# Decode attention with a gated feed-forward on one core: key transposes moved to VectorE in 32x32 blocks, and wider products at the end

## The chip, the cores and the metric

One NeuronCore of a Trainium2 chip runs the whole kernel; the other cores are idle. The metric is device time in microseconds: the median of the runs, lower is better. A profile of one execution comes with it. In what follows PE is TensorE, PEld its weight loads, DVE is VectorE, ACT is ScalarE, POOL is GpSimd and SP is SyncE, which here only issues loads.

## The reference

Two tokens (B = 2) go through one layer: attention over the last 4096 cached positions, 32 query heads on 8 key/value heads of 128, and beside it a gated feed-forward of width 1792. All data is float32.

```python
W = min(4096, max(256, Sk // 4))              # 4096 of 32768 cached positions
xn = _layernorm(x)
q = (xn @ wq).reshape(B, Sq, 32, 128)
scores = einsum("bhqd,bhkd->bhqk", q, k[last W]) * 128 ** -0.5
o = einsum("bhqk,bhkd->bhqd", softmax(scores), v[last W])
attn = o.reshape(B, Sq, 4096) @ wo
gate, up = xn @ W_gate, xn @ W_up
h = (gate * (gate > 0)) * up
return x + attn + h @ W_down
```

Nearly all bytes are read once: wq 8 MB, W_gate, W_up and W_down 3.5 MB each, keys and values 32 MB each, wo 8 MB, 95 MB in all.

## The kernel before, in words

**Loads.** Every large load is issued by SP's queue into a ring of four slots of 32 KB per partition (`RING`, line 17). A slot takes one load of about 4 MB; SP waits at a load until the last reader of its slot is done. In order of the program: x (three small loads, issued by ACT), `wq` in two halves (line 136), `w_gate`, `w_up` (226), and then keys and values. `load_kv` (114) fetches 4096 positions of two heads, 64 partitions for each, one 32 KB row per partition. There are four groups g (two batch rows times two halves of the heads), each with two key and two value loads (a = 0, 1). `load_down` (95) comes as 13 rows per partition and a rest of 128 rows in two small loads into a tile `wx`; `wo` comes in one load of 4 MB and four of 2, 1.25, 0.5 and 0.25 MB (498).

**Start.** Layernorm statistics of x run on DVE and POOL, the normalised row is spread to columns by 16 products (212), and 32 products of 512 columns form q (222). q is transposed and laid out in `qz` (228 to 241). Then the gate and up products run (243 to 257), and h is transposed into `hT` (283 to 293).

**A group.** `transposes` (308) turns the keys on PE, 128x128 at a time, into PSUM; `evacuate` (304) copies four of these at once to the tile `kt`, by turns on ACT and DVE. `scores` (322) multiplies `qz` by `kt`, 512 columns at a time, into four 32-row strips of one PSUM bank. `softmax` (335) takes the maxima, spreads them, runs Exp on ACT over a doubled view, turns the probabilities on PE (373) and masks them on DVE (374). `values` (386) multiplies them by the value tile; `gather` (404) and `finish` (414) sum the parts. `kwork` (432) writes out by hand how PE interleaves a key tile's transposes with the softmax of the group before. The keys of group g are worked ahead of the values of group g - 1, and loads are issued in that order.

**End.** After the last group, `project` (478) multiplies h by `w_down` and the heads by `wo`, each as four products of 128 columns into four strips of `y_ps`; the four late pieces of `wo` let the last products start as each piece lands. `y_ps` is copied to `yo` and stored (501 to 503).

Each engine works in the order of the program; a wait at its head holds all that is behind it.

Of the kernel before, what the change touches and what calls it, by code (L numbers as in the profile page):

```python
# [9 lines left out]
F32 = mybir.dt.float32  # L10
# [10 lines left out]
def kernel(  # L21
# [28 lines left out]
    S1 = W // (Q * 512)  # L50

# [7 lines left out]
    ring = ctx.enter_context(tc.tile_pool(name="ring", bufs=RING))  # L59
    ktp = ctx.enter_context(tc.tile_pool(name="ktp", bufs=2))  # L60
    work = ctx.enter_context(tc.tile_pool(name="work", bufs=2))
    ps_kt = ctx.enter_context(tc.tile_pool(name="ps_kt", bufs=3, space=PSUM))
# [5 lines left out]
    def load(name, src, shape):  # L68
        t = ring.tile(shape, F32, name=name, tag="ring")
        nc.sync.dma_start(t, src)  # L70
        return t


    def load_wq(m):
        src = wq[m * 2 * P:(m + 1) * 2 * P, :].rearrange("(p k) f -> p k f", p=P)
        return load(f"wq{m}", src, [P, 2, HQ * DH])

    def load_ff(w, name):
        return load(name, w.rearrange("(p k) f -> p k f", p=P), [P, KC, F])
# [6 lines left out]
    FM = 13  # L86
    KX = 4
    LEFT = 0
    FX = F - P * FM
    RX = (FX - 8 * LEFT) // (8 * KX)  # L90
    SX = RX + (LEFT > 0)
    MQ = P * FM // Q
    assert 8 * KX * RX + 8 * LEFT == FX

    def load_down():
        t = ring.tile([P, FM, D], F32, name="wd", tag="ring")
        wx = ktp.tile([P, SX, D], F32, name="wx", tag="kT")
        nc.gpsimd.memset(wx[0:64], 0.0)  # L98
        nc.sync.dma_start(
            t.rearrange("p k e -> p (k e)"), w_down[0:P * FM, :].rearrange("(p k) e -> p (k e)", p=P)  # L100
        )
        row = P * FM
        for b in range(2):
            src = bass.AP(
                tensor=w_down.tensor, offset=w_down.offset + row * D,
                ap=[[RX * D, KX], [KX * RX * D, 4], [1, RX * D]],
            )
            nc.sync.dma_start(wx[32 * b:32 * b + 4 * KX, 0:RX].rearrange("p k e -> p (k e)"), src)
            row += 4 * KX * RX
        for i in range(LEFT):  # L110
            nc.sync.dma_start(wx[i:32:4, RX], w_down[row + 8 * i:row + 8 * i + 8, :])
        return t, wx

    def load_kv(cache, name, g, a):
        r, b = divmod(g, B)
        base = cache[b, r * C + 2 * a, SK - W:SK, :]
        run = J * DH
        src = bass.AP(
            tensor=cache.tensor, offset=base.offset, ap=[[run, PK], [SK * DH, 2], [1, run]]
        )  # L120
        return load(f"{name}{g}_{a}", src, [P, run])
# [14 lines left out]
    wqt = [load_wq(m) for m in range(2)]  # L136
# [4 lines left out]
    NSLOT = C * S1  # L141
    qz = const.tile([P, NG, NSLOT * 36], F32, name="qz")
    nc.gpsimd.memset(qz, 0.0)
    ones = const.tile([1, 1], F32, name="ones")
# [4 lines left out]
    hT = const.tile([P, FM + SX, B, 16], F32, name="hT")  # L149
    nc.gpsimd.memset(hT, 0.0)  # L150
    hx = const.tile([32, SX, 64], F32, name="hx")
    nc.gpsimd.memset(hx, 0.0)
# [8 lines left out]
    spread = const.tile([HR, NE, HR, NE], F32, name="spread")  # L161
    nc.gpsimd.memset(spread, 0.0)
    for e in range(NE):
        nc.gpsimd.tensor_copy(spread[:, e, :, e], ident[0:HR, 0:HR])


    pick = const.tile([P, 4, 24], F32, name="pick")
    nc.gpsimd.memset(pick, 0.0)
    nc.vector.tensor_reduce(
        out=pick[:, :, 8:16], in_=ident.rearrange("p (q u k) -> p u k q", q=Q, u=4), op=ALU.add, axis=AX.X  # L170
    )


    HK = 2 * REP
    by_h = const.tile([P, NP, HK], F32, name="by_h")
    nc.vector.tensor_reduce(
        out=by_h, in_=ident.rearrange("p (q a s k) -> p a k q s", q=Q, a=NP, s=S1), op=ALU.add, axis=AX.XY
    )

    half_of = const.tile([P, 2], F32, name="half_of")  # L180
    nc.vector.tensor_reduce(
        out=half_of, in_=ident.rearrange("p (y h) -> p h y", h=2), op=ALU.add, axis=AX.X
    )
    own = const.tile([P, 2, REP], F32, name="own")
    nc.vector.tensor_copy(own, half_of[:, :, None].to_broadcast([P, 2, REP]))
# [22 lines left out]
    xt_ps = ps_1.tile([P, 2, KC, 32], F32, name="xt_ps", tag="misc")  # L208
    for kc in range(KC):
        m, k = divmod(kc, 2)  # L210
        for o, cols in ((0, xn.rearrange("r (m p k) -> r m k p", m=2, k=2)[:, m, k]), (1, xn.rearrange("r (p k) -> r k p", k=KC)[:, kc])):
            nc.tensor.matmul(xt_ps[:, o, kc, :], cols, rep.rearrange("r s b -> r (s b)"), start=True, stop=True)  # L212
    xnT = const.tile([P, 2, KC, 32], F32, name="xnT")
# [4 lines left out]
    for kc in range(KC):  # L218
        for r in range(R):
            for c in range(C):  # L220
                n = r * C + c
                nc.tensor.matmul(  # L222
                    q_ps[r][32 * c:32 * c + 32, :], xnT[:, 0, kc, :], wqt[kc // 2][:, kc % 2, n * 512:(n + 1) * 512],
                    start=(kc == 0), stop=(kc == KC - 1),
                )
    gw = load_ff(w_gate, "wg")
    uw = load_ff(w_up, "wu")
    for r in range(R):
# [3 lines left out]
        for i in range(REP):  # L232
            nc.tensor.transpose(
                qt[:, i].rearrange("p c s b -> p (c s b)"), qs[:, i * P:(i + 1) * P], ident
            )
        for b in range(B):
            dst = qz[:, r * B + b].rearrange("p (a s h k) -> p a s h k", a=NP, s=S1, h=2)
            for h in range(2):
                nc.vector.tensor_copy(
                    dst[:, :, :, h, 0:REP], qt[:, :, h::2, 0:S1, b].rearrange("p i a s -> p a s i")  # L240
                )
# [4 lines left out]
    x_ps = ps_1.tile([32, 2, FX], F32, name="x_ps", tag="o0")  # L246
    for h, dst, wt in ((0, g_ps, gw), (1, u_ps, uw)):
        for kc in range(KC):
            for c in range(Q):
                nc.tensor.matmul(  # L250
                    dst[32 * c:32 * c + 32, :], xnT[:, 1, kc, :], wt[:, kc, c * MQ:(c + 1) * MQ],
                    start=(kc == 0), stop=(kc == KC - 1),
                )
        for kc in range(KC):
            nc.tensor.matmul(
                x_ps[:, h], xnT[:, 1, kc, :], wt[:, kc, Q * MQ:], start=(kc == 0), stop=(kc == KC - 1)
            )
# [9 lines left out]
    gx = work.tile([32, 2, FX], F32, name="gx", tag="qs")  # L267
    nc.scalar.copy(gx[:, 0], x_ps[:, 0])
    nc.vector.scalar_tensor_tensor(gx[:, 1], gx[:, 0], 0.0, gx[:, 0], op0=ALU.is_gt, op1=ALU.mult)
    part = 4 * KX * RX  # L270
    for b in range(2):
        g_in, u_in = (
            a[:, b * part:(b + 1) * part].rearrange("p (j e s) -> p e j s", j=4, e=KX) for a in (gx[:, 1], x_ps[:, 1])
        )
        nc.vector.tensor_tensor(
            hx[:, 0:RX, 32 * b:32 * b + 4 * KX].rearrange("p s (e j) -> p e j s", j=4), g_in, u_in, op=ALU.mult
        )
    for i in range(LEFT):
        lo = 2 * part + 8 * i
        nc.vector.tensor_tensor(  # L280
            hx[:, RX, i:32:4], gx[:, 1, lo:lo + 8], x_ps[:, 1, lo:lo + 8], op=ALU.mult
        )
    ht_ps = ps_1.tile([P, FM + SX, B], F32, name="ht_ps", tag="misc")
    for k in range(FM):
        for c in range(Q):
            nc.tensor.matmul(
                ht_ps[32 * c:32 * c + 32, k], hh[:, k], ident[:, 32 * c:32 * c + B], start=True, stop=True
            )
    for k in range(SX):
        m = 64 if k < RX else 32  # L290
        nc.tensor.matmul(ht_ps[0:m, FM + k], hx[:, k, 0:m], ident[0:32, 0:B], start=True, stop=True)
    nc.vector.tensor_copy(hT[:, 0:FM, :, 0], ht_ps[:, 0:FM])
    nc.vector.tensor_copy(hT[0:64, FM:FM + RX, :, 0], ht_ps[0:64, FM:FM + RX])
    if LEFT:
        nc.vector.tensor_copy(hT[0:32, FM + RX, :, 0], ht_ps[0:32, FM + RX])
# [3 lines left out]
    HW = W // S1  # L299
    ss, pts, rls = {}, {}, {}  # L300
    kts, osb = {}, {}
    turn = [0]

    def evacuate(dst, src):
        (nc.vector.tensor_copy if turn[0] % 2 else nc.scalar.copy)(dst, src)  # L305
        turn[0] += 1

    def transposes(g, a, s1, kt_in):

        kt = ktp.tile([P, 2, HW], F32, name=f"kT{g}_{a}_{s1}", tag="kT")  # L310
        kts[g, a, s1] = kt
        for n in range(2 * Q):
            pk = ps_kt.tile([P, 512], F32, name=f"pk{g}_{a}_{s1}_{n}", tag="kt")
            for u in range(4):
                j = 8 * Q * s1 + 4 * n + u
                nc.tensor.transpose(pk[:, u * P:(u + 1) * P], kt_in[:, j * P:(j + 1) * P], ident)  # L316
            evacuate(
# [214 lines left out]
```

## Time and profile before

| | |
|---|---|
| median of 3 runs | 231.29 us (231.12 to 231.61) |
| the profiled execution | 231.43 us, its span 229.6 us |
| PE, PEld, DVE, ACT busy | 185.4, 114.7, 67.2, 46.9 us |
| bytes read | 94.90 MB, 413 GB/s over the span |
| instructions | 4149, of them 1876 matmuls and 1876 weight loads |

The span runs from the first to the last instruction; 1.8 us of the execution lie outside it. A busy PE is not a PE at its peak, since matmuls overlap one another. "DMA share" is the mean busy share of the 16 DMA engines. A float32 product is two matmul instructions in the rows (a transpose is one).

### The profile page before, as it was taken

What the parts mean: (1) busy time and instruction counts of PE and PEld (TensorE: products, weight loads), DVE (VectorE), ACT (ScalarE), POOL (GpSimd) and SP (SyncE); (2) the same over time, 40 slices, a digit from 0 to 9 for tenths busy, and PEclk for the clock granted to TensorE, in tenths of its full rate; (3) what the DMA queues carried; (4) which work ended last, traced back from release to release, by engine and by line L of the source; (5) the groups of instructions that cost most, each with busy time, mean ns of one, the idle gap of its engine ahead of it and who ended that gap; (6) DMA issues with size and microseconds to landing.
All of it is one profiled execution on the core that took longest, in us unless ns stands there. A gap on an engine that the chain in (4) does not pass through costs nothing.

```text
span 229.6 us, 4149 instructions
## 1 busy us (share of the span) xinstructions
PE 185.4 (81%) x1876; PEld 114.7 (50%) x1876; DVE 67.2 (29%) x135; ACT 46.9 (20%) x80; POOL 8.2 (4%) x25
## 2 busy tenths in 40 slices
PE   0059961779999899997799699889979973988794
PEld 0052231259666583663484566458446532247682
DVE  0320021034444570441472143157124224001000
ACT  0020100004344451440351233045023202010000
POOL 8100000000000000000000000000000300000000
PEclk9999999577999999999999799999999999599678
DMA  7999999999999999999999999999999999999981
GB/s 274 451 428 408 454 410 437 422 451 442 405 425 451 415 417 445 442 411 420 457 417 432 428 440 414 434 445 414 422 440 437 417 428 440 423 442 414 410 364 49
DMA packets 3824, 95.15 MB, mean 414 GB/s; under 512 B 434, under 2 KB 448, under 8 KB 704
## 3 DMA queue, kind: packets, MB, share of 16 engines
q1 hardware_dynamic: 3796, 94.90, 96.7%
q8 instruction: 14, 0.23, 0.4%
q14 instruction: 2, 0.02, 0.0%
q10 hardware_dynamic: 12, 0.00, 0.0%
HBM read 94.90 MB, written 0.00 MB: 413 GB/s over the span
## 4 chain that ended last, share of the span: by engine, by line
DMA 54%; PE 41%; DVE 2%; issue 1%; ACT 1%; ACTq 0%; POOL 0%; DVEq 0%
DMA k<-in_A_k_cache_dram 37%; PE pk L316 21%; DMA wo<-in_A_wo_dram 13%; PE s L329 7%; PE y_ps L480 5%; DMA x<-in_A_x_dram 4%; PE o L393 3%; PE q_ps L222 3%; PE xt_ps L212 2%; ACT p L362 1%; PE pp L373 0%; ACTq L135 0%; PE oa L409 0%; DVE stats L189 0%; DVE kT L305 0%
## 5 line engine op out<-in xcount | busy, mean ns | idle before, releaser
L316 PE MATMUL pk<-ident,k 128*128 128x128 f32 x512 | 67.9, 286 | 6.0 <-DMA k<-in_A_k_cache_dram 5.9
L316 PEld LDWEIGHTS pk<-ident,k 128*128 128x128 f32 x512 | 57.9, 146 | 20.9 <-issue 16.7
L305 DVE COPY kT<-pk 128x512 f32<-128x512 f32 x64 | 44.2, 691 | 52.1 <-PE pk L316 46.2
L305 ACT COPY kT<-pk 128x512 f32<-128x512 f32 x64 | 37.5, 585 | 69.5 <-PE pk L316 69.5
L393 PE MATMUL o<-v,pt 128*32 128x512 f32 x256 | 32.5, 641 | 0.0
L329 PE MATMUL s<-kT,qz 128*32 128x512 f32 x256 | 30.9, 598 | 0.0
L393 PEld LDWEIGHTS o<-v,pt 128*32 128x32 f32 x256 | 11.3, 117 | 15.7 <-issue 10.9
L212 PE MATMUL xt_ps<-rep,xn 2*128 2x32 f32 x16 | 3.7, 400 | 13.9 <-DVE xn L206 13.9
L329 PEld LDWEIGHTS s<-kT,qz 128*32 128x32 f32 x256 | 7.1, 109 | 11.9 <-issue 11.5
L305 DVE COPY on<-o 128x512 f32<-128x512 f32 x4 | 2.8, 692 | 30.5 <-PE o L393 30.5
L409 PE MATMUL oa<-on,pick 128*16 128x128 f32 x64 | 8.3, 273 | 4.1 <-DVE on L305 3.3
L480 PE MATMUL y_ps<-wo,oT 128*17 128x128 f32 x256 | 10.3, 329 | 1.6 <-DMA wo<-in_A_wo_dram 1.6
L409 PEld LDWEIGHTS oa<-on,pick 128*16 128x16 f32 x64 | 5.8, 97 | 11.3 <-DVE on L305 7.0
L250 PE MATMUL u_ps<-wu,xnT 128*32 128x416 f32 x32 | 5.8, 901 | 6.1 <-DMA wu<-in_B_W_up_dram 6.1
L212 PEld LDWEIGHTS xt_ps<-rep,xn 2*128 2x128 f32 x16 | 3.6, 320 | 13.9 <-issue 13.9
L222 PE MATMUL q_ps<-wq,xnT 128*32 128x512 f32 x64 | 9.7, 777 | 0.5 <-DVE xnT L214 0.5
L480 PEld LDWEIGHTS y_ps<-wo,oT 128*17 128x17 f32 x256 | 8.1, 119 | 3.6 <-DMA wo<-in_A_wo_dram 2.6
L305 ACT COPY on<-o 128x512 f32<-128x512 f32 x4 | 2.3, 586 | 27.0 <-PE o L393 27.0
L98 POOL MEMSET wx<- 64x2048 f32 x1 | 1.8, 1804 | 169.1 <-PE s L329 169.1
L362 ACT ACTIVATE p<-s,nm 128x1024 f32<-128x1024 f32 x4 | 4.5, 1114 | 13.1 <-DVE nm L357 13.1
L374 DVE TENSOR_TENSOR pt<-pp,own 128x512 f32<-128x512 f32 x8 | 5.4, 689 | 2.6 <-PE pp L373 2.6
L373 PE MATMUL pp<-ident,p 128*128 128x128 f32 x32 | 4.9, 280 | 1.7 <-ACT p L362 1.5
(83 smaller groups left out, 68.2 us busy)
## 6 DMA issues: line engine op xcount, KB each, us to landing
k<-in_A_k_cache_dram SPq DMA_DIRECT2D x8, 4096.0 KB, 23.9
v<-in_A_v_cache_dram SPq DMA_DIRECT2D x8, 4096.0 KB, 28.3
wq<-in_A_wq_dram SPq DMA_DIRECT2D x2, 4096.0 KB, 21.7
wo<-in_A_wo_dram SPq DMA_DIRECT2D x1, 4096.0 KB
wg<-in_B_W_gate_dram SPq DMA_DIRECT2D x1, 3584.0 KB, 29.8
wu<-in_B_W_up_dram SPq DMA_DIRECT2D x1, 3584.0 KB, 39.3
wd<-in_B_W_down_dram SPq DMA_DIRECT2D x1, 3328.0 KB
wo<-in_A_wo_dram SPq DMA_DIRECT2D x1, 2048.0 KB
```

Source lines behind the costliest of these rows:

```text
L212: nc.tensor.matmul(xt_ps[:, o, kc, :], cols, rep.rearrange("r s b -> r (s b)"), start=True, stop=True)
L222: nc.tensor.matmul(q_ps[r][32 * c:32 * c + 32, :], xnT[:, 0, kc, :], wqt[kc // 2][:, kc % 2, n * 512:(n + 1) * 512], start=(kc == 0), stop ...
L250: nc.tensor.matmul(dst[32 * c:32 * c + 32, :], xnT[:, 1, kc, :], wt[:, kc, c * MQ:(c + 1) * MQ], start=(kc == 0), stop=(kc == KC - 1),)
L305: (nc.vector.tensor_copy if turn[0] % 2 else nc.scalar.copy)(dst, src)
L316: nc.tensor.transpose(pk[:, u * P:(u + 1) * P], kt_in[:, j * P:(j + 1) * P], ident)
L329: nc.tensor.matmul(ss[g][32 * q:32 * q + 32, :], qz[:, g, 32 * n:32 * n + 32], kt[:, h, q * 512:(q + 1) * 512], start=(a == 0 and s1 == 0 ...
L362: nc.scalar.activation(p, both, AF.Exp, bias=nm, scale=SCALE, accum_out=l)
L373: nc.tensor.transpose(pp[:, u], pv[:, lo:lo + P], ident)
L374: nc.vector.tensor_tensor(pts[g][:, jh].rearrange("p n u k -> p u n k"), pp.rearrange("p u (n k) -> p u n k", k=HK), own.rearrange("p h i ...
L393: nc.tensor.matmul(o[32 * q:32 * q + 32, :], pts[g][:, jh, n].rearrange("p u k -> p (u k)"), v[:, lo:lo + 512], start=(s1 == 0 and jh == 0 ...
L409: nc.tensor.matmul(oa[g], pick[:, u, 8 - 8 * a:24 - 8 * a], ons[a][:, u], start=(a == 0 and u == 0), stop=(a == NP - 1 and u == 3),)
L480: nc.tensor.matmul(y_ps[32 * e:32 * e + 17, :], lhsT.rearrange("p b s -> p (b s)")[:, 0:17], w[:, e * P:(e + 1) * P], start=False, stop=stop,)
```

## The change: what it does

- **Keys.** PE no longer turns keys. DVE transposes each key tile in 32x32 blocks, four instructions of 128x2048 elements for each load, from the ring straight into `kt`. `qz` is laid out to fit (new `spot`, `qT`, `rq` and 16 small copies for each half of the heads); `scores` runs in four 32-row strips, two at a time.
- **Probabilities.** Exp runs over 512 columns, not 1024. Two products with a permutation (`perm`) put the rows in order, and one DVE transpose of 128x1024 writes `pts`. A mask now follows the value products (`gather`, on DVE), and one product, not four, gathers them; `finish` adds a reduction.
- **Order.** Within one loop step a group's keys and values are loaded k, k, v, v and worked in that order. `keep_busy` adds two PE products without a use at each group's start. `kwork` and the interleaving are gone.
- **Ring.** One tile of the same size, cut by `place`. `wq` is one load of 64 KB per partition over two slots; `w_down` is one load of 14 rows per partition, so that `wx`, `hx` and `x_ps` go. The first half of `wo` comes in two loads.
- **End.** Products with `w_down` and most of `wo` have 512 columns, each into the next of four 32-row strips of `y4` (`slot`). `y4` is copied by DVE and folded into `y_ps` by four products; the last eight products of `wo` keep four times 128 columns (`quarters`). x is loaded again (`xr`).

```diff
-    def load_wq(m):
-        src = wq[m * 2 * P:(m + 1) * 2 * P, :].rearrange("(p k) f -> p k f", p=P)
+    ring = const.tile([P, RING * RW], F32, name="ring")
+    def place(cols):
+        lo = taken[0] % RING * RW
+        taken[0] += -(-cols // RW)
+        return ring[:, lo:lo + cols]
+    def load_rows(w):
+        t = place(KC * w.shape[1])
+        nc.sync.dma_start(t, w.rearrange("(p k) f -> p (k f)", p=P))
...
+    def scores(g, a, kt_in):
+        for s1 in range(S1):
+            kt = ktp.tile([P, JH, CB, KL, 2], F32, name=f"kT{g}_{a}_{s1}", tag="kT")
+            for n in range(2):
+                lo = JH // 2 * n
+                j = JH * s1 + lo
+                nc.vector.transpose(
+                    kt[:, lo:lo + JH // 2].rearrange("p j c k h -> p (j c k h)"),
+                    kt_in[:, j * DH:(j + JH // 2) * DH],
+                )
+            for cb in range(CB):
+                for h in range(2):
+                    lo = 32 * (2 * s1 + h)
+                    nc.tensor.matmul(ss[g][lo:lo + 32, :], qz[:, g, cb, h, 16 * a:16 * a + 32], kt[:, :, cb, :, h], ...)
...
+    def turn(g, p, l):
+        pp = ps_kt.tile([P, 2, 512], F32, name=f"pp{g}", tag="kt")
+        for h in range(2):
+            nc.tensor.matmul(pp[:, h], perm[:, h], p, start=True, stop=True)
+        pts[g] = work.tile([P, NP * S1, JH, HK], F32, name=f"pt{g}", tag="pt", bufs=1)
+        nc.vector.transpose(pts[g].rearrange("p n j k -> p j n k"), pp.rearrange("p h y -> p y h"))
...
+    for g in range(NG):
+        kt_in = [load_kv(k_cache, g, a) for a in range(NP)]
+        v_in = [load_kv(v_cache, g, a) for a in range(NP)]
+        if g:
+            keep_busy(g - 1)
+        scores(g, 0, kt_in[0])
+        if g > B and g % B == 1:
+            take_heads(g // B - 1, op)
+        if g:
+            gather(g - 1, NP - 1)
+        scores(g, 1, kt_in[1])
+        if g:
+            finish(g - 1)
+        turn(g, *softmax(g, maxima(g)))
+        values(g, 0, v_in[0])
+        gather(g, 0)
+        values(g, 1, v_in[1])
+        if g % B == 0 and g:
+            op = spread_heads(g // B - 1, ps_kt, "kt")
+    dw = load_down()
...
+    cuts = {0: (0, NJ // 2, NJ), 1: (0, 8, 13, 15, NJ)}
+    EARLY = FM + NJ + cuts[1][1]
+    def slot(lhsT, w):
+        t, i = done[0] % Q, done[0]
+        nc.tensor.matmul(
+            y4[32 * t:32 * t + 32, :], lhsT.rearrange("p b s -> p (b s)"), w, start=(i < Q), stop=(i >= EARLY - Q)
+        )
+        done[0] += 1
...
+    down(0, Q)
+    op = spread_heads(R - 1, ps_1, "misc")
+    down(Q, 2 * Q)
+    take_heads(R - 1, op)
+    for r in range(R):
+        wt = place(NJ * D).rearrange("p (j e) -> p j e", j=NJ)
+        for j0, j1 in zip(cuts[r], cuts[r][1:]):
+            nc.sync.dma_start(wt[:, j0:j1], wo_rows(r, j0, j1))
+        if r == R - 1:
+            down(2 * Q, FM)
+        for j in range(NJ):
+            if (r, j) < (1, cuts[1][1]):
+                slot(oT[:, r, j], wt[:, j])
+                continue
+            if j == cuts[1][1]:
+                ys = work.tile([P, D], F32, name="ys", tag="qs")
+                nc.vector.tensor_copy(ys, y4)
+                quarters(fold[:, 0:17], ys, False)
+            quarters(oT[:, r, j].rearrange("p b s -> p (b s)")[:, 0:17], wt[:, j], (r, j) == (R - 1, NJ - 1))
```

More of the change, by code (lines that the diff above doesn't have):

```diff
@@ L95, in load_down @@
[L95 to L112, printed above, removed]
@@ L159 @@
     nc.gpsimd.tensor_copy(rep, ident[0:B, None, 0:B].to_broadcast([B, 16, B]))
-    spread = const.tile([HR, NE, HR, NE], F32, name="spread")
+    spread = const.tile([HR, P + NE], F32, name="spread")
     nc.gpsimd.memset(spread, 0.0)
[L163 to L168, printed above, removed]
+    nc.gpsimd.tensor_copy(spread[:, NE - 1:NE - 1 + P:NE], ident[0:HR, 0:HR])
+    mask = const.tile([P, 4], F32, name="mask")
@@ L278 @@
[L278 to L283, printed above, removed]
-    for k in range(FM):
-        for c in range(Q):
+    ht_ps = ps_1.tile([32, FM * Q, B], F32, name="ht_ps", tag="misc")
+    firsts = ident.rearrange("p (c r) -> p c r", c=Q)[:, :, 0:B]
+    for k in range(FM):
+        nc.tensor.matmul(ht_ps[:, k * Q:(k + 1) * Q], hh[:, k], firsts, start=True, stop=True)
@@ L292 @@
[L292 to L317, printed above, removed]
-                kt[:, :, n * 256:(n + 1) * 256], pk.rearrange("p (y h) -> p h y", h=2),
-            )
-            yield
```

328 lines of the change are left out of this document (142 added, 186 removed).

## The prediction

> **What bounds the kernel now.** I read the page's head first, then busy time by stretches of the span, then the timeline of the last microseconds, and the chain of waits for the start.
>
> ```profile
> span 229.6 us, 4149 instructions
> ...
> PE 185.4 (81%) x1876; PEld 114.7 (50%) x1876; DVE 67.2 (29%) x135; ACT 46.9 (20%) x80; POOL 8.2 (4%) x25
> ...
> q1 hardware_dynamic: 3796, 94.90, 96.7%
> q8 instruction: 14, 0.23, 0.4%
> ```
>
> PE is 81% busy, which looks like a bound. But the load queue q1 fills 96.7% of the 16 DMA engines' span. The stretches decide (columns: length, each engine's busy time with its count, PE clock, DMA share, GB/s).
>
> ```profile
> 39.00:206.00 167.00, 148.77 (x1327) 91.67 (x1331) 59.81 (x106) 44.57 (x77) 1.80 (x1) 0.94 1.00 429
> ...
> 221.00:222.00 1.00, 1.00 (x36) 0.90 (x32) 0.00 (x0) 0.00 (x0) 0.00 (x0) 0.75 0.94 385
> 222.00:223.00 1.00, 1.00 (x48) 0.98 (x40) 0.00 (x0) 0.00 (x0) 0.00 (x0) 1.00 0.75 309
> 223.00:224.00 1.00, 1.00 (x48) 0.94 (x36) 0.00 (x0) 0.00 (x0) 0.00 (x0) 1.00 0.73 283
> 224.00:225.00 1.00, 0.97 (x40) 0.74 (x32) 0.00 (x0) 0.00 (x0) 0.00 (x0) 1.00 0.51 199
> 225.00:226.00 1.00, 1.00 (x37) 0.62 (x28) 0.00 (x0) 0.00 (x0) 0.00 (x0) 1.00 0.13 47
> ```
>
> From 39 to 206 us the DMA share is 1.00 at 429 GB/s: no hole is left for faster compute to fill. Compute off the loads' path is worth nothing there; what can move is the head, the tail and the work of the DMA engines themselves. The tail has something odd: from 221 the share falls 0.94, 0.75, 0.73, 0.51, 0.13. The engines do not end together.
>
> ```profile
> 216.27 10.35 PE L480 MATMUL y_ps<-wo,oT 128*17 128x128 f32 x256 [1.57 <-DMA wo<-in_A_wo_dram]
> 224.26 1.01 PEld L480 LDWEIGHTS y_ps<-wo,oT 128*17 128x17 f32 x40 [0.31 <-DMA wo<-in_A_wo_dram]
> 225.55 0.35 PEld L480 LDWEIGHTS y_ps<-wo,oT 128*17 128x17 f32 x16 [0.28 <-DMA wo<-in_A_wo_dram]
> 226.20 0.13 PEld L480 LDWEIGHTS y_ps<-wo,oT 128*17 128x17 f32 x8 [0.30 <-DMA wo<-in_A_wo_dram]
> 226.69 0.29 DVE L502 COPY yo<-y_ps 128x128 f32<-128x128 f32 x1 [11.73 <-PE y_ps L480]
> 227.00 0.60 SPq L503 DMA_DIRECT2D out_dram<-yo  x1
> ```
>
> PE waits for each of the last three pieces of `wo`; the last lands at 226.2, and only 3.4 us of products, copy and store follow. A load lands when the slowest of 16 engines has its share. The shares missing from 221 to 226.2 sum to 0.06 + 0.25 + 0.27 + 0.49 + 0.87 + 0.2 = 2.1 us: the mean engine was done 2.1 us before the last.
>
> **The change part by part.**
>
> **Keys on DVE (gain 0, covered).** Removed: 512 PE transposes and the 128 copies behind them. The rows are from the groups (busy, mean ns).
>
> ```profile
> L316 PE MATMUL pk<-ident,k 128*128 128x128 f32 x512 | 67.9, 286 | 6.0 <-DMA k<-in_A_k_cache_dram 5.9
> ...
> L338 DVE TENSOR_REDUCE m<-s 128x1 f32<-128x512 f32 x4 | 2.8, 691 | 4.8 <-PE s L329 4.8
> ...
> L261 DVE SCALAR_TENSOR_TENSOR gr<-gs 128x416 f32<-128x416 f32 x1 | 0.6, 592 | 4.5 <-ACT gs L259 4.5
> ```
>
> Added: 4 DVE transposes of 2048 elements per key load, 32 in all. No trace row has one. Between 416 and 512 elements DVE's time grows by 99 ns for 96, about 1.04 ns each over 0.16 us fixed, so 2.3 us; I take that. Ends: nothing faster than half of it, and double, 4.6 us. At 2.3 a key load costs DVE 9.2 us, a group 18.4 us, and with mask, sums, maxima and the turn (1.2 us for 1024 elements) about 24 us, against 16.8 MB at 429 GB/s = 39.1 us of loading. The cover ends at (39.1 - 5.3) / 8 = 4.2 us a transpose.
>
> **Ring order and waits (0, covered).**
>
> ```profile
> k<-in_A_k_cache_dram SPq DMA_DIRECT2D x8, 4096.0 KB, 23.9
> v<-in_A_v_cache_dram SPq DMA_DIRECT2D x8, 4096.0 KB, 28.3
> ```
>
> A load takes 9.8 us alone and lands 24 to 28 us after its issue: SP runs two loads ahead. After: with the first key load of a group landing at T, its slot is free at T+9.2 and is due at T+29. The value slot is the tight one: second keys at T+9.8, transposes to T+19, scores, softmax about 7 us, `values` 4 to 6 us: free by T+33 to T+41, due at T+49. New wait: the mask in `gather` holds DVE until `values` has read a value load; behind it stand only the next group's transposes, whose load lands later. Scores alternate between two strips, not four; at worst a pair costs 0.6 us (L329's mean instruction), 9.6 us per key load, about its loading time and still inside those covers.
>
> **Start (0, covered).**
>
> ```profile
> 1.58 8.89 DMA x<-in_A_x_dram
> ...
> 18.14 6.35 PE q_ps L222 x32
> 24.48 0.02 issue
> 24.50 26.72 DMA k<-in_A_k_cache_dram
> ```
>
> x comes in small loads that share engines with `wq`. If its waits double with 64 KB rows, it lands at 19.4, not 10.5; half of the 16 spreading products go (-1.8 us), so q starts at about 25, and the first key load is issued at 32, not 24.5. The load took 26.7 us for 9.8 of transfer, so some 17 us of that is queue; 7 us later still leaves 10. Longer `qz` work (`rq`, 16 small copies) hides before the keys land at 51.
>
> **Extra x load, `keep_busy`, more small DVE work (0).** `xr` holds PE at its first use, with all tail products behind it; the last Exp comes near 51.2 + 3 x 39.1 + 22 = 190, the x loads at the start took 8.9 us, and `w_down`, which the tail needs first, lands 8 MB of `wo`, 19.6 us, ahead of the end, near 206. POOL loses its memset for `wx`, for which SP's queue waited; the queue ran two loads ahead then too.
>
> **Instruction stream (-1.4).** The matmul count falls from 1876 to about 950: transposes -528, tail products -244, h transposes -86, gathers -48, feed-forward rest, spreads and maxima -48; `rq` and `keep_busy` +28. Weight loads fall as much, so fetches fall from 14 to about 7. Those 14 packets took 0.4% of 16 engines over 229.6 us: 14.7 engine-us, 1.05 us each, on one engine each. With 14 some engine can have two and some none; with 7 none needs two. One packet is worth at least 1.05 us, and at most 1.9: the mean engine holds 0.9 packets, the last two, and this difference of 1.1 covers the 2.1 us. I take 1.4, as part of the 2.1 must stem from the unequal start.
>
> **`w_down` (+0.6).** `wx`, 256 KB in two loads of 16 rows, joins the even load. If `wx` lay evenly, this costs 0; if only on engines that did not end last, the last one now carries 1/16 of it, 16 KB at 429/16 GB/s = 0.6. The last engine here is late by fetches, so I take 0.6.
>
> The Trainium skill, "DMA: Bandwidth & Descriptors", section "Why a DMA increments its semaphore by 16 and not by 1", says that a load uses as many engines, up to 16, as divide its pattern's slowest dimension. By it `wx` (slowest dimension 4) lay on four engines and the cost is 0.6; spread evenly the sum would be -1.4. No row here shows `wx` by engine.
>
> **`wo` (0) and the end (0).** 512 columns save no PE time: two instructions at 0.12 each against eight at 0.025.
>
> ```profile
> 195.47 6.37 PE L393 MATMUL o<-v,pt 128*32 128x512 f32 x32
> ...
> 203.50 3.60 PE L393 MATMUL o<-v,pt 128*32 128x512 f32 x29
> ...
> 218.00:220.00 2.00, 2.00 (x44) 1.63 (x40) 0.00 (x0) 0.00 (x0) 0.00 (x0) 0.50 0.97 398
> ```
>
> At full clock a 512-column instruction steps in 0.12 us (29 in 3.60), at half clock 0.20; 128-column ones 0.025 (x40 in 222:223, clock 1.00) and 0.05 (x40 here, 0.50). `wo`'s 2 MB piece lands 1.25 MB, 3.1 us, ahead of 224.2, so now near 220.4; 8 products 1.9, drain 0.3, copy of `y4` 0.7, fold 0.2: 223.5, as the 1.25 MB piece lands.
>
> **Sum.** -1.4 + 0.6 = -0.8 on the profiled 231.43 (229.6 of span and 1.8 around it): 230.6. That execution lies 0.14 over the median, 231.29, so 230.5.
>
> **The rivals.**
> *Nothing moves.* The fetch is worth 1.05 (net -0.45), or as many engines keep a double fetch and PE is late by 0.5 at the end. 230.9 to 231.8, centre 231.2. For it: the deficit has other parts. Against it: half of all instructions go.
> *PE at half clock at the end (slower).* PE has less to do and rests between the halves of `wo`.
>
> ```profile
> 126.00:128.00 2.00, 1.05 (x12) 0.13 (x4) 0.00 (x0) 0.58 (x1) 0.00 (x0) 1.00 1.05 442
> 128.00:130.00 2.00, 0.88 (x5) 0.91 (x6) 0.00 (x0) 0.00 (x0) 0.00 (x0) 0.84 0.99 426
> ```
>
> A rest of about 2 us here brought 0.50 next. With 0.50 held from 220.4: 8 products 3.2, drain, copy, fold 1.4, then 40 + 16 + 8 instructions at 0.05 = 3.2: 228.2, against 225.4 + 0.4. That is 1.8 behind the old end of products, 233.1; it decides if the half clock lasts past about 222. Against it: six `w_down` products stand between the `wo` parts, 28 instructions from about 215.8, and in the profile before PE rose within 5.5 us of 216.27. The Trainium skill, "TensorE: Matmul & The Clock Gate", section "What's actually happening", gives one window of about 3.4 us for either change of clock; by it a 1.5 us rest keeps the clock and this rival falls. The trace disagrees: the fall above needed only 2 us.
> *DVE is the bound.* At 4.6 us a transpose a group takes 42.1: 51.2 + 4 x 42.1 = 219.6, then softmax, values and all tail products, some 17 us: 237. The Trainium skill, "VectorE: DVE Perf Modes", section "The three transpose paths", gives 311 ns for 128x128 in bf16, one element a cycle; no run here shows it.
> *The change fails its purpose:* one ring tile waits as a whole, so loads run one group at a time. Each group would expose some 15 us, 290 in all. Against: PE waits for `wo` piece by piece inside one tile.
>
> **How the numbers follow.** Forecast 0.58 (own range 229.9 to 231.0), nothing moves 0.23, half clock 0.11, DVE 0.04, whole-tile waits 0.04. 0.2%, 0.46 us, is about what this measurement can tell. Faster: 0.53 of the forecast's and 0.02 of the second case's, 0.55; same 0.05 + 0.19 = 0.24; slower 0.02 + 0.11 + 0.04 + 0.04 = 0.21. Range: down to 229.7 (a fetch worth 1.9 and no `wx` cost gives 229.4, the outermost bound), up to 232.4, which takes in the near half of the half-clock case.
>
> **What would show it.** DMA share 1.00 from 39 to 206; about 7 instruction packets; the share's fall at the end shorter by near 1 us; DVE transposes of 2.3 us; PE waiting for each of the last `wo` pieces. Wrong: a DMA share under 0.97 in mid-span, PE clock 0.50 after 222, or 12 or more instruction packets.

## The result and the profile after

The changed kernel takes 229.82 us (median of 6 runs, 229.75 to 230.01) against 231.26 us (231.12 to 231.61) for the one before: a ratio of 0.9938, with a 95% interval of 0.9925 to 0.995. That is 1.44 us less. The forecast was 230.5, 0.8 us less, within 229.7 to 232.4. The profiled execution took 229.95 us. Below, a time is the median of all executions of a kernel and a ratio is taken over its faster ones alone, which matters for e5 and e12, whose executions spread by 2 and 4%.

From the head of the page of the kernel after:

```profile
span 228.1 us, 2217 instructions
PE 155.2 (68%) x952; PEld 50.5 (22%) x952; DVE 102.2 (45%) x121; ACT 8.3 (4%) x27; POOL 6.4 (3%) x24
q1 hardware_dynamic: 3756, 94.90, 97.1%
q8 instruction: 7, 0.11, 0.2%
```

PE lost 30 us of work and 924 of its matmuls, ACT lost 39 us, DVE gained 35, and the span moved by 1.5 us. q8 is the queue whose packets fetch instructions: 14 before, 7 now.

Busy time by stretches of the kernel after (same columns as before: length, PE, PEld, DVE, ACT, POOL, PE clock, DMA share, GB/s):

```profile
39.00:206.00 167.00, 126.99 (x702) 38.17 (x700) 93.50 (x91) 5.05 (x17) 0.00 (x0) 0.93 1.00 430
...
221.00:222.00 1.00, 0.82 (x8) 0.00 (x0) 0.05 (x1) 0.00 (x0) 0.00 (x0) 1.00 0.98 397
222.00:223.00 1.00, 0.31 (x12) 0.23 (x16) 0.64 (x1) 0.00 (x0) 0.00 (x0) 1.00 0.73 289
223.00:224.00 1.00, 1.00 (x44) 0.92 (x40) 0.00 (x0) 0.00 (x0) 0.00 (x0) 1.00 0.41 162
224.00:225.00 1.00, 1.00 (x32) 0.48 (x24) 0.00 (x0) 0.00 (x0) 0.00 (x0) 1.00 0.04 16
```

The middle is as it was: share 1.00 at 430 GB/s (1.00 and 429 before). All that moved is at the end. (A packet is counted in the slice in which it starts, so that a share can pass 1.) The loads' share now falls within three slices, to 0.04 by 224; before it was still 0.51 there and 0.13 a slice later.

Timeline of the end, kernel after (start, length, instruction, in brackets the engine's idle time before it and what ended that):

```profile
214.91 1.92 PE L438 MATMUL y<-ring,oT 128*32 128x512 f32 x16 [1.80 <-DMA ring<-in_A_wo_dram]
...
219.90 1.92 PE L438 MATMUL y<-ring,oT 128*32 128x512 f32 x16 [1.36 <-DMA ring<-in_A_wo_dram]
...
224.14 0.35 PEld L445 LDWEIGHTS y_ps<-ring,oT 128*17 128x17 f32 x16 [0.22 <-DMA ring<-in_A_wo_dram]
224.77 0.13 PEld L445 LDWEIGHTS y_ps<-ring,oT 128*17 128x17 f32 x8 [0.28 <-DMA ring<-in_A_wo_dram]
225.25 0.29 DVE L476 COPY yo<-y_ps 128x128 f32<-128x128 f32 x1 [2.61 <-PE y_ps L445]
225.56 0.69 SPq L477 DMA_DIRECT2D out_dram<-yo  x1
```

The last wait for a piece of `wo` ends at 224.77; before it was 226.20. Copy and store follow as before (225.25 and 225.56 for 226.69 and 227.00). So the last load landed 1.43 us earlier, and this is the whole gain.

The costliest DVE groups of the kernel after (busy us, mean ns | idle before, its releaser):

```profile
L294 DVE STREAM_TRANSPOSE kT<-ring 128x2048 f32<-128x2048 f32 x32 | 71.0, 2278 | 12.1 <-DMA ring<-in_A_k_cache_dram 12.0
L367 DVE TENSOR_TENSOR on<-o,mask 128x512 f32<-128x512 f32 x8 | 5.4, 679 | 21.3 <-PE o L358 21.3
L345 DVE STREAM_TRANSPOSE pt<-pp 128x1024 f32<-128x1024 f32 x4 | 5.0, 1250 | 13.9 <-PE pp L343 13.9
...
L316 DVE TENSOR_REDUCE m<-s 128x1 f32<-128x512 f32 x4 | 2.8, 692 | 12.7 <-PE s L301 12.7
```

A transpose takes 2.28 us, as estimated. The right-hand column holds something the forecast left out: DVE waits for PE 21.3 + 13.9 + 12.7 = 47.9 us, 12.0 a group, and for keys only 12.0 us in all, 3.0 a group.

### The profile page after: what moved, and what is told of

It reads as the page before. It is cut to its first block, busy times and chain, and to the rows that moved or that the text cites. A ratio compares the mean times of both kernels' runs of the same rounds, so it can differ in the third digit from the quotient of the medians.

```text
span 228.1 us, 2217 instructions
## 1 busy us (share of the span) xinstructions
PE 155.2 (68%) x952; PEld 50.5 (22%) x952; DVE 102.2 (45%) x121; ACT 8.3 (4%) x27; POOL 6.4 (3%) x24
## 4 chain that ended last, share of the span: by engine, by line
DMA 58%; DVE 20%; PE 16%; issue 4%; ACT 1%; ACTq 0%; DVEq 0%
DMA ring<-in_A_k_cache_dram 39%; DVE kT L294 16%; DMA ring<-in_A_wq_dram 10%; DMA ring<-in_A_wo_dram 9%; PE q_ps L221 4%; PE g_ps L258 2%; PE s L301 2%; PE u_ps L258 1%; PE rq L239 1%; PE y_ps L445 1%; PE pp L343 1%; PE o L358 1%; PE y L438 1%; PE qt L232 1%; DVE qz L248 1%
## 5 line engine op out<-in xcount | busy, mean ns | idle before, releaser
L294 DVE STREAM_TRANSPOSE kT<-ring 128x2048 f32<-128x2048 f32 x32 | 71.0, 2278 | 12.1 <-DMA ring<-in_A_k_cache_dram 12.0
L301 PE MATMUL s<-kT,qz 128*32 128x512 f32 x256 | 60.3, 626 | 19.3 <-DVE kT L294 19.3
L358 PE MATMUL o<-ring,pt 128*32 128x512 f32 x256 | 33.9, 628 | 4.8 <-DVE rl L349 4.8
L301 PEld LDWEIGHTS s<-kT,qz 128*32 128x32 f32 x256 | 13.6, 111 | 65.0 <-issue 32.9
L367 DVE TENSOR_TENSOR on<-o,mask 128x512 f32<-128x512 f32 x8 | 5.4, 679 | 21.3 <-PE o L358 21.3
L358 PEld LDWEIGHTS o<-ring,pt 128*32 128x32 f32 x256 | 9.8, 114 | 22.1 <-issue 16.8
L343 PE MATMUL pp<-p,perm 128*128 128x512 f32 x16 | 10.1, 766 | 4.5 <-ACT p L337 4.5
L345 DVE STREAM_TRANSPOSE pt<-pp 128x1024 f32<-128x1024 f32 x4 | 5.0, 1250 | 13.9 <-PE pp L343 13.9
L221 PE MATMUL q_ps<-ring,xnT 128*32 128x512 f32 x64 | 9.5, 759 | 2.1 <-DMA ring<-in_A_wq_dram 2.1
L373 PE MATMUL oa<-on,picks 128*16 128x512 f32 x16 | 8.3, 597 | 3.8 <-DVE on L367 3.8
L316 DVE TENSOR_REDUCE m<-s 128x1 f32<-128x512 f32 x4 | 2.8, 692 | 12.7 <-PE s L301 12.7
L438 PE MATMUL y<-ring,oT 128*32 128x512 f32 x48 | 5.7, 596 | 3.2 <-DMA ring<-in_A_wo_dram 3.2
L309 PE MATMUL idle<-pt,ident 128*128 128x512 f32 x12 | 6.0, 618 | 0.0
```

The source lines that it names most:

```text
L221: nc.tensor.matmul(q_ps[r][32 * c:32 * c + 32, :], xnT[:, kc, :], wqt[:, kc, n * 512:(n + 1) * 512], start=(kc == 0), stop=(kc == KC - 1),)
L294: nc.vector.transpose(kt[:, lo:lo + JH // 2].rearrange("p j c k h -> p (j c k h)"), kt_in[:, j * DH:(j + JH // 2) * DH],)
L301: nc.tensor.matmul(ss[g][lo:lo + 32, :], qz[:, g, cb, h, 16 * a:16 * a + 32], kt[:, :, cb, :, h], start=(a == 0 and cb == 0), stop=(a == N ...
L309: nc.tensor.matmul(idle, ident, pts[g][:, 2 * n:2 * n + 2].rearrange("p n j k -> p (n j k)"), start=True, stop=True)
L343: nc.tensor.matmul(pp[:, h], perm[:, h], p, start=True, stop=True)
L345: nc.vector.transpose(pts[g].rearrange("p n j k -> p j n k"), pp.rearrange("p h y -> p y h"))
```

## The experiments

The theory: the gain is the instruction stream. Fewer packets of instructions mean that the slowest DMA engine ends earlier. Rivals: the shapes of the loads (64 KB rows for `wq`, `w_down` in one load); the shorter tail; a PE that is quicker at the end. Ratios below are against the kernel before, with 95% intervals. A label such as e1 names a run.

### More instructions, the same work

Products of two columns without a use, put behind each `scores` call, fill the stream and move no data. Three amounts were run.

```diff
+    def filler(g, a):
+        few = ps_1.tile([32, 2], F32, name=f"few{g}_{a}", tag="misc")
+        for _ in range(56):                      # e1: 56; e2: 16; e9: 8
+            nc.tensor.matmul(few, ident[:, 0:32], ident[:, 0:2], start=True, stop=True)
...
         scores(g, 0, kt_in[0])
+        filler(g, 0)
...
         scores(g, 1, kt_in[1])
+        filler(g, 1)
```

56 a call (e1):

> The changed kernel with 448 tiny products without a use (32x32 by 2 columns), 56 behind each key tile's scores: 1792 more instructions, so about 14 instruction packets as before the change; loads, DVE and the tail stay. Theory (the end is set by the DMA engine that carries most instruction packets): 1.3 to 2.0 us later than the changed kernel's 229.82, so 231.1 to 231.8, with the last wo piece late by as much. Rival 1 (the gain came from the shapes of the loads): 229.8. Rival 2 (from less PE work in the tail): 229.8, as the tail is untouched.

232.4 us, ratio 1.0062 (1.0035 to 1.0089), with 14 packets: later than the 231.1 to 231.8 expected, and less steady than the others (231.68 to 235.15). Stretches and timeline of its end:

```profile
224.00:225.00 1.00, 1.00 (x8) 0.12 (x2) 0.00 (x0) 0.00 (x0) 0.00 (x0) 1.00 0.41 166
225.00:226.00 1.00, 0.14 (x6) 0.03 (x7) 0.69 (x1) 0.00 (x0) 0.00 (x0) 1.00 0.18 70
```

```profile
226.09 1.75 PEld L452 LDWEIGHTS y_ps<-ring,oT 128*17 128x17 f32 x64
228.20 0.29 DVE L483 COPY yo<-y_ps 128x128 f32<-128x128 f32 x1 [2.28 <-PE y_ps L452]
```

The loads end late again, about as in the kernel before (share 0.41 and 0.18, where the kernel after has 0.04 in the first of these slices). But all 64 last weight loads run without a wait for `wo`: PE is later still, by itself, so the time of this run mixes two causes. Two smaller amounts stay clear of that.

16 a call (e2):

> The same with 128 tiny products, 512 instructions: about 9 packets, two more than the changed kernel. Theory in its sharp form (packets go round a set of 8 engines, and the ninth is the first to meet an engine twice): most of the step at once, 230.9 to 231.5. Theory in its plain form (the delay grows with the count): 2/7 of the step, 230.2 to 230.4. Rivals 1 and 2: 229.8.

231.24 us, ratio 1.0005 (0.9986 to 1.0024). The whole gain is gone with two more packets. From its page, its stretches and its timeline:

```profile
q8 instruction: 9, 0.15, 0.3%
```

```profile
223.00:224.00 1.00, 1.00 (x42) 0.82 (x32) 0.00 (x0) 0.00 (x0) 0.00 (x0) 1.00 0.48 176
224.00:225.00 1.00, 0.10 (x4) 0.00 (x0) 0.00 (x0) 0.00 (x0) 0.00 (x0) 1.00 0.06 12
```

```profile
225.44 0.35 PEld L452 LDWEIGHTS y_ps<-ring,oT 128*17 128x17 f32 x16 [1.62 <-DMA ring<-in_A_wo_dram]
226.07 0.13 PEld L452 LDWEIGHTS y_ps<-ring,oT 128*17 128x17 f32 x8 [0.28 <-DMA ring<-in_A_wo_dram]
```

At 224 the share is 0.06, which is one engine of sixteen. PE does nothing for 1.62 us until this one engine has brought its share: here the tail is a single late engine.

8 a call (e9):

> The changed kernel with 64 tiny products without a use, 8 behind each key tile's scores: 256 more instructions, about 8 packets, one fewer than the padded kernel that lost the whole gain. Theory in its sharp form (eight packets meet eight engines once each): 229.8 to 230.0, no step. If the added products themselves cost the time: 230.5.

230.0 us, ratio 0.9947 (0.9934 to 0.996). From its page:

```profile
span 228.2 us, 2477 instructions
...
q8 instruction: 8, 0.13, 0.2%
```

Seven packets 229.82, eight 230.0, nine 231.24. The step of 1.24 us lies between eight and nine.

The traces show why. They keep the time at which each DMA engine's share of a load landed, sixteen shares for an evenly spread load. For the last piece of `wo` (us; in brackets the number of shares):

| run | packets | shares of the last piece, in groups |
|---|---|---|
| after | 7 | 222.82 to 223.17 (8), 223.76 (1), 224.16 to 224.72 (7) |
| e9 | 8 | 222.72 to 223.21 (7), 223.93 (1), 224.31 to 224.70 (8) |
| e2 | 9 | 222.66 to 223.24 (7), 223.96 (1), 224.17 to 224.63 (7), 226.03 (1) |
| e1 | 14 | 222.74 to 223.14 (7), 223.84 (1), 224.41 and 224.69 (2), 225.80 to 226.19 (6) |

With seven packets seven shares are about 1.5 us late, with eight eight; the ninth packet makes one of these eight late a second time, and 14 packets are 2 + 6 x 2. So the packets go round eight of the sixteen engines, and the load ends with the engine that had most of them. (One share of the other eight is late by 0.7 to 0.9 us in all four runs; no run here shows why.) Nor is it only that a packet comes late: in e1 twelve packets were fetched by 193 us, and four shares of the first load of `wo` already land 1.5 us behind four others (211.06 to 211.46 against 209.58 to 209.94). A packet itself runs 1.02 to 1.11 us, but its engine loses some 1.5: in e2 the packets of `wo` just behind the ninth fetch run longer, 0.44 us for 4 KB where the others take 0.16.

### The same products in one place

e5:

> The changed kernel with 450 tiny products without a use, 150 at the head of each of the groups 1 to 3, where PE waits for DVE's first key transposes: about 14 instruction packets, but none of the added work between the scores and the softmax. Theory: the last wo piece lands near 226.2, as in the kernel before and in the first padded kernel, and PE is in time: 231.1 to 231.5. Rival (padding costs through late products of PE, not through the loads): either 232.4 again or 229.8.

```diff
     def keep_busy(g):
+        few = ps_1.tile([32, 2], F32, name=f"few{g}", tag="misc")
+        for _ in range(150):
+            nc.tensor.matmul(few, ident[:, 0:32], ident[:, 0:2], start=True, stop=True)
```

256.05 us, ratio 1.1029 (1.0986 to 1.1072), where 231.1 to 231.5 was expected: a miss. As a test of packets it failed. Its timeline shows another thing:

```profile
89.56 14.02 PE L309 MATMUL few<-ident 128*32 128x2 f32 x300
...
112.38 4.51 DVE L294 STREAM_TRANSPOSE kT<-ring 128x2048 f32<-128x2048 f32 x2 [8.42 <-PE s L301]
```

300 instructions at 47 ns hold PE for 14 us at the start of a group; the scores stand behind them, DVE waits 8.4 us for the scores, and so the slots come free late. The kernel has little room inside a group.

### The shapes of the loads

`wq` again as two loads of 32 KB rows (e3):

> The changed kernel with wq in two loads of 32 KB rows in place of one of 64 KB rows. Theory: x lands near 10.5 us as before the change, not 15.3, and the time stays within 0.3 us of 229.8. Rival 1: most of the 1.4 us comes back, 230.8 to 231.3.

```diff
-    wqt = load_rows(wq)
+    wqt = place(KC * HQ * DH)
+    for m in range(2):
+        cols = slice(m * 2 * HQ * DH, (m + 1) * 2 * HQ * DH)
+        nc.sync.dma_start(wqt[:, cols], wq.rearrange("(p k) f -> p (k f)", p=P)[:, cols])
+    wqt = wqt.rearrange("p (k f) -> p k f", k=KC)
```

229.98 us, ratio 0.9939 (0.9926 to 0.9952): as after. The first work on x, in the timeline of the kernel after and then of this one:

```profile
15.29 0.68 DVE L187 BATCH_NORM_STATS2 stats<-x 2x6 f32<-2x512 f32 x1 [12.81 <-DMA x<-in_A_x_dram]
```

```profile
10.26 0.68 DVE L191 BATCH_NORM_STATS2 stats<-x 2x6 f32<-2x512 f32 x1 [7.78 <-DMA x<-in_A_x_dram]
```

The 64 KB rows delay x by 5.0 us, and it costs nothing: the shape of `wq`'s load falls as a cause.

`w_down`'s 14th row in a load of its own, with a pattern whose slowest dimension is 2 (e4):

> The changed kernel with w_down's 14th row of each partition (128 rows of 2 KB, 256 KB) in a second load whose source pattern has a slowest dimension of 2. Theory, with the rule that a load uses as many engines as divide its slowest dimension: two engines carry 64 rows of 2 KB each, 5.4 us, all others 0.7 us less, and the end comes 2.8 us later if neither has an instruction packet, 4.7 if one has: 232.6 to 234.5. Rival (a load spreads evenly whatever its pattern, or late engines are made up for): 229.8 to 230.0.

```diff
-        nc.sync.dma_start(t, w_down.rearrange("(p k) e -> p (k e)", p=P))
+        main = (FM - 1) * D
+        nc.sync.dma_start(t[:, 0:main], w_down.rearrange("(p k) e -> p (k e)", p=P)[:, 0:main])
+        src = bass.AP(tensor=w_down.tensor, offset=w_down.offset + main,
+            ap=[[P // 2 * FM * D, 2], [FM * D, P // 2], [1, D]])      # e6: [[FM * D, 2], [2 * FM * D, P // 2], [1, D]]
+        nc.sync.dma_start(t[:, main:FM * D], src)
```

230.07 us, ratio 0.9945 (0.9933 to 0.9957): a miss, nothing happened. The two dimensions here are one run of 128 evenly spaced rows, and they can be joined. The same with rows interleaved, which can't be joined (e6; the 14th rows land in another order, so the output differs from the reference):

> w_down's 14th rows once more in a second load of 256 KB, now with a source pattern of two interleaved runs that can't be joined into one dimension (it puts these rows in another order, so the output is not the reference's). Rule that a load uses as many engines as divide its slowest dimension: 2 engines carry 64 rows each, the end comes 2.8 us later if neither has an instruction packet, 4.7 if one has: 232.6 to 234.5. Rival (a load spreads evenly whatever its pattern): 230.1, as with the joinable pattern.

235.15 us, ratio 1.0171 (1.0158 to 1.0184), 5.3 us over the kernel after and later than the 232.6 to 234.5 of the rule. Its stretches:

```profile
224.00:225.00 1.00, 0.00 (x0) 0.00 (x0) 0.00 (x0) 0.00 (x0) 0.00 (x0) 1.00 0.56 223
225.00:226.00 1.00, 0.85 (x8) 0.34 (x12) 0.00 (x0) 0.00 (x0) 0.00 (x0) 1.00 0.28 113
226.00:227.00 1.00, 1.00 (x12) 0.16 (x4) 0.00 (x0) 0.00 (x0) 0.00 (x0) 1.00 0.22 78
227.00:228.00 1.00, 0.12 (x8) 0.06 (x8) 0.69 (x1) 0.00 (x0) 0.00 (x0) 1.00 0.11 45
```

The share ends at 0.11, two engines of sixteen. 256 KB on two engines are 128 KB each, 4.9 us at the 429/16 GB/s of one engine, against 0.6 spread evenly: 4.3 of the 5.3; the rest is not explained. The load was due before all of `wo`, and its two engines are still late when the others have ended, since no engine rests in between: two shares of the last piece land at 229.87 and 229.90, the other fourteen by 226.20. The Trainium skill's rule on the slowest dimension ("DMA: Bandwidth & Descriptors", "Why a DMA increments its semaphore by 16 and not by 1") holds for this pattern: only two shares of the small load land, at 210.41 and 210.48. In e4, with the pattern that can be joined, sixteen land one after another, from 203.04 to 205.13: an even spread.

The 14th rows as 16 loads of 8 partitions (e8):

> The changed kernel with w_down's 14th rows in 16 loads of 8 partitions (16 KB each), the rest in one load of 13 rows for each partition. Theory: each small load lies on the same eight engines, which get 0.7 us more, the other eight 0.7 us less. If the instruction packets fall on the other eight, the end comes 0.6 us earlier: 229.2. If they fall on these eight, or on both: 230.4. Rival (the end does not hang on single engines): 229.8 to 230.0.

```diff
...
+        for p in range(0, P, 8):
+            nc.sync.dma_start(t[p:p + 8, main:], rows[p:p + 8, main:])
```

236.41 us, ratio 1.022 (1.0207 to 1.0233): a miss. SP's timeline, then one of its stretches:

```profile
176.61 30.87 SPq L98 DMA_DIRECT2D ring<-in_B_W_down_dram  x16
207.58 2.86 SPq L466 DMA_DIRECT2D ring<-in_A_wo_dram  x6
```

```profile
204.00:206.00 2.00, 1.15 (x12) 0.62 (x16) 0.86 (x2) 0.00 (x0) 0.00 (x0) 1.00 0.14 33
```

SP was held 30.9 us at the 16 small loads, `wo` was issued only at 207.6, and the DMA engines had nothing to do meanwhile. Why SP was held is open, and the run says nothing on how the last rows lie over the engines. It shows one packet alone, though: the pause let all engines begin `wo` level, fifteen shares of its last piece land from 229.34 to 229.58, and the sixteenth, after one more fetch at 223.8, at 230.75.

The kernel before with `wx`'s rows in one dimension of 16 (e10):

> The kernel before with wx's rows in plain order, 16 rows in one dimension, so that each of its two loads lies on 16 engines and not on four. Theory, term of 0.6 for w_down: the engine that ends last carried none of wx and now carries 16 KB, 231.9. If the four engines that carried wx were the last ones: 230.5 to 231.3.

```diff
-                ap=[[RX * D, KX], [KX * RX * D, 4], [1, RX * D]],
+                ap=[[RX * D, 4 * KX], [1, RX * D]],
...
```

234.7 us, ratio 1.016 (1.0141 to 1.0178): a miss, and slower. Stretches of this kernel, then of the kernel before:

```profile
200.00:204.00 4.00, 3.23 (x28) 1.23 (x24) 0.00 (x0) 0.59 (x1) 0.00 (x0) 0.81 1.10 371
204.00:208.00 4.00, 3.43 (x32) 1.40 (x24) 0.48 (x1) 0.00 (x0) 0.00 (x0) 1.00 1.09 288
```

```profile
200.00:204.00 4.00, 3.23 (x28) 1.32 (x24) 0.00 (x0) 0.58 (x1) 0.00 (x0) 0.87 1.02 437
204.00:208.00 4.00, 3.17 (x30) 1.28 (x23) 0.69 (x1) 0.00 (x0) 0.00 (x0) 1.00 1.02 436
```

The engines are as busy and move 371 and 288 GB/s in place of 437 and 436. Each `wx` load goes to 16 adjacent partitions, in the kernel before as well; new is that all engines write there at once, not four. Their 8 KB packets take 0.31 to 0.95 us, where with four engines each took 0.31 or 0.32, and the large packets beside them are slower too (32 KB: 1.93 us, else 1.22). Why, no run here shows. The Trainium skill, "SBUF — State Buffer", section "Door 1: The DMA port swizzle", says that a transfer's rate depends on how many of the memory's ports its partitions reach, and by its mapping 16 adjacent ones reach few; that would fit. For `w_down`'s term the run decides nothing.

The trace of the kernel before says more. Its last piece of `wo` lands in three groups: 222.25 to 222.82 (4 shares), 223.90 to 224.25 (3) and 225.13 to 226.16 (9). The `wx` loads land in four shares each, the second at 205.48, 205.59, 205.85 and 206.40; shares that keep the distance of one engine's loads follow at the first load of `wo` (215.20, 215.32, 215.57, 216.14) and at its last piece (225.13, 225.25, 225.50, 226.07). So four of the nine late shares are the engines of `wx`, and the other five are engines with two packets, the last of them at 226.16. Two things held the kernel before at the same time, 0.09 us apart: double fetches on one set of engines and `wx` on another. Fewer packets alone would have brought about 0.1 us; it also took the new load of `w_down`, which spreads `wx`'s bytes over all engines. This is worked out from the landing times; the fitting run would be the kernel after with `wx` as before, and it was not made.

### The tail

The kernel before with 512-column products for `w_down` and most of `wo`, as after (e11, shortened):

> The kernel before with the changed kernel's tail alone: w_down and the first 24 wo products of 512 columns in four strips, folded by four products. 430 fewer instructions, about 12 packets. Theory, sharp form: still more than 8, some engine has two, 231.1 to 231.5. Plain form (delay grows with the count): 2/7 of the step less, 230.7 to 231.0. Rival 2 (the gain came from the tail's products): 229.8 to 230.3.

```diff
     for k in range(FM):
-        project(hT[:, k], dw[:, k], False)
+        slot(hT[:, k], dw[:, k])
...
         for j in range(NJ):
+            if (r, j) < (1, 8):
+                slot(oT[:, r, j], wt[:, j])
+                continue
```

230.96 us, ratio 0.9988 (0.998 to 0.9997), with 13 packets. The tail alone brings 0.3 of 1.44 us, and all of it by the loads: the last share lands at 225.82, 0.34 us earlier than before. So the tail's products fall as a cause. By the same distances that last share belongs to an engine of `wx`, and the engines with two packets are done by 225.56: here `wx` sets the end, and what the step from 14 to 13 packets is worth can't be read from the time.

Six `w_down` products moved ahead of `wo`, so that no filler stands between its parts (e7):

> The changed kernel with the last six w_down products moved ahead of wo, so that PE rests about 3 us between the two parts of wo (from 216 to 219.9). Prediction's half-clock rival: the clock stands at 0.50 when the 2 MB piece lands, 8 products take 3.2 us in place of 1.9 and the last 64 instructions 0.05 each: products end near 227.7, 232.3 in all. If the clock holds: 229.8.

```diff
-    down(Q, 2 * Q)
+    down(Q, FM)
...
-        if r == R - 1:
-            down(2 * Q, FM)
```

229.98 us, ratio 0.9942 (0.9931 to 0.9954). PE's clock row in 40 slices, in tenths:

```profile
PEclk9999997697699999889967999995699999589999
```

It ends at 9999. In the profiled execution PE's rest before the second part of `wo` was no longer than in the kernel after, as its other products ran later, so the run is a weak test of a long rest (0.92 us, 1.36 in the kernel after). It does show that the order of these products isn't needed.

### How near DVE is to the bound

Every key transpose twice (e12):

> The changed kernel with every key transpose done twice, so that a transpose costs DVE 4.56 us and a group 36.5 + 5.3 = 41.8 us, over the 39.1 us of its loads. Prediction: the cover ends at 4.2 us, so the loads begin to wait and the end comes 3 to 7 us later, 233 to 237. If the cover is wider than worked out: 229.8 to 230.5.

```diff
-                nc.vector.transpose(
-                    kt[:, lo:lo + JH // 2].rearrange("p j c k h -> p (j c k h)"),
-                    kt_in[:, j * DH:(j + JH // 2) * DH],
-                )
+                for _ in range(2):
+                    nc.vector.transpose(
+                        kt[:, lo:lo + JH // 2].rearrange("p j c k h -> p (j c k h)"),
+                        kt_in[:, j * DH:(j + JH // 2) * DH],
+                    )
```

300.41 us, ratio 1.2805 (1.2736 to 1.2874), where 233 to 237 was expected: a miss by about 60 us. Its DVE groups and SP's timeline:

```profile
L295 DVE STREAM_TRANSPOSE kT<-ring 128x2048 f32<-128x2048 f32 x64 | 144.9, 2294 | 1.1
L368 DVE TENSOR_TENSOR on<-o,mask 128x512 f32<-128x512 f32 x8 | 5.4, 679 | 25.8 <-PE o L359 25.8
```

```profile
122.94 19.29 SPq L106 DMA_DIRECT2D ring<-in_A_k_cache_dram  x2
180.37 19.29 SPq L106 DMA_DIRECT2D ring<-in_A_k_cache_dram  x2
```

From one group's key loads to the next's lie 57.4 us, not 39.1. The keys take 144.9/4 = 36.2 of these; the other 21 are DVE's remaining work and its waits for PE, which don't lie beside the transposes but behind them. DVE no longer waits for keys (1.1 us in all): DVE, with the work of PE that it waits for, is the bound. Had only its busy time counted, as the forecast and this run's expectation had it, a group would have been some 42 us.

## Why the prediction was right, and where it was not

**The bound** was read rightly: share 1.00 from 39 to 206 us before and after, and 30 us less on PE moved nothing there.

**Instruction stream (-1.4) and `w_down` (+0.6).** The packets fell to 7 as forecast, and the mechanism holds: before, the engine that landed last had fetched twice, and now none has. The sum was too small, -0.8 for -1.44. The landing times give each term. Before, the three shares with one packet land at 224.13 on average and the five with two at 225.77: the second packet costs 1.6 us (1.5 in e1), where the forecast took 1.4 from a range of 1.05 to 1.9. After, the seven shares with one packet land at 224.50 on average, 0.4 later: that is `w_down`, with whatever else moves all engines alike, forecast 0.6. Together -1.2. The other 0.2 are spread inside the groups, the last share lying 0.4 over its group's mean before and 0.2 now. So both terms were a little off, each by 0.2, to the same side. `wq`'s rows are not the reason (e3).

Two parts of the working did not hold. The 2.1 us that were read as the distance from the mean engine to the last are 1.6 by the landing times (226.16 less a mean of 224.58): the shares count a packet where it starts, and their sum takes in the 0.4 us between the end of the last packet (225.73) and its landing. The mean itself came 0.9 us earlier, which the forecast left out. And `w_down` was priced as a cost alone. That `wx` lay "only on engines that did not end last" was right by 0.09 us; had it stayed there, the fetches would have gained next to nothing. That the forecast came out so near is in this part luck.

**Keys on DVE (0).** The price was right (2.28 us for 2.3), the gain of nothing too, so the rival of a bound on DVE fell at 229.8. The cover was wrong. The step "the cover ends at (39.1 - 5.3) / 8 = 4.2 us a transpose" took DVE's other work as all that stands beside the transposes. DVE's waits for PE in the softmax and the values, 12.0 us a group, stand there as well. What is left is its wait for keys, at most 3.0 us a group, 0.4 us for each transpose: the cover ends near 2.7 us, not 4.2. e12 went past it; in e1 and e5 the added work of PE used it up, and DVE's waits for keys fell from 12.0 us to 1.8 and 4.8 in all. The DVE rival was therefore closer than its 0.04: by this estimate half a microsecond more for each transpose would have made DVE, with its waits for PE, the bound.

The Trainium skill, "VectorE: DVE Perf Modes", section "The three transpose paths", gives 311 ns for 128x128 in bf16. That is 2.4 ns for each of a partition's 128 elements, and scaled by elements it would make a key transpose 5.0 us, an estimate. The longer float32 rows here take less than half of that: 1.11 ns an element in the key transposes (2278 ns for 2048 elements) and 1.22 in the one of 1024.

**Start (0).** x came at 15.3 us, not the 19.4 of the worst case, and nothing was paid (e3). The timeline has the issue of the first key loads (start, length on SP's queue):

```profile
28.89 3.97 SPq L106 DMA_DIRECT2D ring<-in_A_k_cache_dram  x2
```

28.9, where 24.5 was before and 32 was the bound: inside the cover of 10 us.

**`wo` and the end (0).** Behind drain, copy and fold the next products start at 222.92, 0.06 us after the 1.25 MB piece has landed (222.86), as near as forecast. So PE no longer waits for that piece, but for the 2 MB one and the last two, and the forecast's sign of a wait for each piece holds for these three. e11 leaves nothing for the tail's products. (The forecast's 0.025 for a 128-column instruction is taken from the 40 weight loads in 222:223; that row has 48 products, 0.021 each. Nothing hangs on it.)

**The rivals.** *Nothing moves* (231.2): fell; the packet above eight is worth 1.24 us in time and some 1.5 on its engine, more than the 1.05 it took. *Half clock at the end* (233.1): fell. In the kernel after PE rested 1.80 us before 214.91 and 1.36 us before 219.90, and the clock stayed at 1.00 to the end. The Trainium skill's single window of about 3.4 us ("TensorE: Matmul & The Clock Gate", "What's actually happening") agrees with that, although the fall after 128 us in the profile before came after a rest of only 2 us (2.07 before 129.12; the clock is 0.50 from 130 to 132). *Whole-tile waits*: PE still waits piece by piece.

## What to carry to other kernels

Where loads fill every DMA engine, look at how the engines end: the distance from the mean engine to the last is what an even end would be worth (1.6 us here before the change, 1.0 after), and instruction packets and small loads on few engines are what makes it uneven. Look at every engine that is late: with one cause gone, the next can stand right behind it, here at 0.09 us. A load that is not spread is paid at the end, however early it was issued. An engine's cover is its idle time in the profile after, waits for other engines left out; the loading time less its busy time is too much, since a round trip through another engine can't be filled with work that comes after it.

## What the runs showed of the hardware that was not expected

- Fetched instructions come in 16 KB packets of about 1.05 us that go round eight of the sixteen DMA engines. Each delays its engine's loads by some 1.5 us, and the cost goes in steps: 7 or 8 packets cost the same within 0.2 us, the ninth 1.24 us.
- Sixteen small loads held the issuing queue 30.9 us (e8).
- Two loads into 16 adjacent partitions each, spread over all engines in place of four, brought the rate from 437 to 371 and 288 GB/s while the engines stayed busy (share 1.10 and 1.09, e10): a full share is not a full rate.
- A source of two dimensions that can be joined was spread as one of 128 rows (e4, sixteen shares, 230.07 us), an interleaved one lay on two engines (e6, 235.15 us).
